# An attention and feed-forward kernel on one core: the order of the first six head pairs, three borrowed buffers, and an earlier load of the last rows

## The chip, the core and the metric

The kernel runs on one core of a Trainium2 chip. A core has TensorE (matrix products), VectorE, ScalarE and GpSimd (elementwise work and reductions), each with its own instruction queue, and SyncE, which here only issues DMAs. Engines run side by side and wait for one another through semaphores; each queue is worked off in order. In the profile's rows they are PE (PEld for its weight loads), DVE, ACT, POOL and SP. The metric is the time of one execution in microseconds (us), as the median of several runs.

## The reference

```python
def rmsnorm(x, g):
    rms = np.sqrt(np.mean(x * x, axis=-1, keepdims=True) + 1e-06)
    return x / rms * g
q_n, k_n = (rmsnorm(q, g_q), rmsnorm(k, g_k))           # (8, 12, 448, 64) each
scores = np.matmul(q_n, k_n.transpose(0, 1, 3, 2)) / np.sqrt(64)
attn = softmax(scores)                                  # max taken off, 1e-09 added to the sum
attn_out = np.matmul(attn, v)
x = attn_out.transpose(0, 2, 1, 3).reshape(8 * 448, 768)
xn = x / np.sqrt(np.mean(x * x, -1, keepdims=True) + 1e-06) * rms_g
g = xn @ w_gate                                         # 768 x 1536
out = (g / (1 + np.exp(-g)) * (xn @ w_val)) @ w_out     # w_out 1536 x 768
```

[...] 

## The kernel before, in words

A sequence has 12 heads, worked on as 6 pairs; there are 48 pairs in all, and the loop of the main program runs over them with the number g. A head's 448 rows are three full tiles of 128, and a rest of 64. The rests of all pairs of a sequence are loaded together (`load_rests`, L430): query rests in one half of the partitions, key rests in the other.

For each pair: `load_pair` (L409, L412) loads the full tiles of q and k. `squares` (L478, L481) squares them on ScalarE and sums on VectorE; `rms_qk` (L497, L498) takes the power -0.5 on GpSimd; `norm_q` (L503) scales the query, on VectorE for pairs 0 and 1 and on GpSimd from pair 2 on. Keys are not scaled: their factor goes into the scale of the exponential. `norm_rests` (L446 to L458) does squares, sums, power and scaling of the rests of two or three pairs at a time. `turn(g, i)` (L519, L523) transposes query (i = 0, with the rest) or key (i = 1) on TensorE; ScalarE copies the turned query qT (L524) and VectorE the turned key kT (L525 its last 64 columns, L527 the others). `score` (L537, L541) multiplies, and ScalarE takes the exponentials; `rests` (L567 to L582) does the 64 last keys and opens the accumulation of the values av (L573) and, for the first seven pairs, of the denominators den (L578). `values` (L589) and `sums` (L602) finish them; VectorE takes the reciprocal (L606) and the product x (L617). av has a single PSUM buffer, so pair g's av starts after pair g - 1's product.

The order on every engine is written out by hand. `pe(fn)` counts a step of TensorE, runs fn, and then all that is due; `after(n, fn)` makes fn due n steps later.

The first seven pairs have no feed-forward work beside them. From pair 7 on, `fill` puts feed-forward products (ff) between the attention steps: L1109 for sequence 0, L991 for its output, L890 and L1081 for the sequences after it, which save products by sums of blocks.

The weights are converted in 72 pieces, one per `convert()`, a pipeline by turns: turn n loads raw piece n (L719), splits piece n - 3 on ScalarE (`split`, L728 and L729), joins piece n - 4 on VectorE (`join`, L734 to L736), adds piece n - 5 on GpSimd into its slot w (L773), and stores piece n - 7 (L761). raw has 7 buffers, top (between split and add) has 4. Before the change the first pairs have four turns at g = 0, and three at each of g = 1 to 6, mostly one by one: one ahead of the next pair's turning, one behind the values, one at the end. From pair 7 on each feed-forward item brings a turn.

Of the kernel before, what the change touches and what calls it, by code (L numbers as in the profile page):

```python
# [8 lines left out]
F32 = mybir.dt.float32  # L9
I32 = mybir.dt.int32  # L10
# [15 lines left out]
BW = 384  # L26
# [309 lines left out]
def safe_scores(  # L336
# [63 lines left out]

    FULL, LAST = slice(0, NK * 128), slice(NK * 128, S)

    def load_pair(g):

        if g >= NG:
            return
        b, hp = divmod(g, NPAIR)
        qk = st["qk", g] = qk_pool.tile([128, 2, 2 * NK * D], F32, name="qk")
        nc.sync.dma_start(out=qk[:, 0].rearrange("p (h n) -> p h n", h=2),  # L409
                          in_=q[b, 2 * hp:2 * hp + 2, FULL].rearrange("h (p t) d -> p h (t d)", t=NK))  # L410
        for h in range(2):
            nc.sync.dma_start(out=qk[:, 1].rearrange("p (t h d) -> p h t d", h=2, d=D)[:, 1 - h],  # L412
                              in_=k[b, 2 * hp + h, FULL].rearrange("(p t) d -> p t d", t=NK))

# [24 lines left out]
    def norm_rests(b, lo, hi):  # L439

        if b >= B:
            return
        n = hi - lo
        rest = st["rest", b][:, lo:hi]
        sq = tmp.tile([128, n, 2, D], F32, name="sq", tag="sq", bufs=2)
        nc.scalar.activation(sq, rest, ACT.Square)  # L446
        ms = small.tile([128, n, 2], F32, name="msr")
        after(1, lambda: nc.vector.tensor_reduce(out=ms, in_=sq, axis=AX_X, op=ALU.add))

        first = b == lo == 0  # L450

        def root():
            nc.gpsimd.tensor_scalar(ms, ms, D * 1e-6, None, ALU.add)
            nc.gpsimd.tensor_tensor(ms, ms, mhalf[:, 0:2 * n].rearrange("p (n h) -> p n h", h=2), ALU.pow)

        def scale():

            (nc.vector if first else nc.gpsimd).tensor_tensor(rest, rest, ms.unsqueeze(3).to_broadcast([128, n, 2, D]), ALU.mult)  # L458

        after(1 if b == 0 else 2, root)  # L460
        if first:
            return scale
        after(1 if b == 0 else 2, scale)

    def direct(g):

# [2 lines left out]
    def squares(g, i):  # L469

        if g >= NG:
            return
        n = 2 * NK
        if i == 0:
            st["ms", g] = small.tile([128, 2 * n], F32, name="ms")
        ms = st["ms", g]
        sq = tmp.tile([128, n * D], F32, name="sq", tag="sq", bufs=2)
        nc.scalar.activation(sq, st["qk", g][:, i], ACT.Square)  # L478

        def reduce():  # L480
            nc.vector.tensor_reduce(out=ms[:, i * n:(i + 1) * n], in_=sq.rearrange("p (n d) -> p n d", d=D), axis=AX_X, op=ALU.add)  # L481

        after(1, reduce)
        if g <= 1:

            after(1, lambda: rms_qk(g, slice(i * n, (i + 1) * n)))
            if i == 0:
                after(1, lambda: norm_q(g))
        elif i == 1:
            after(2, lambda: rms_qk(g))  # L490
            after(2, lambda: norm_q(g))

    def rms_qk(g, cols=slice(0, 4 * NK)):
        if ("rs", g) not in st:
            st["rs", g] = small.tile([128, 4 * NK], F32, name="rs")
        ms = st["ms", g][:, cols]
        nc.gpsimd.tensor_scalar(ms, ms, D * 1e-6, None, ALU.add)  # L497
        nc.gpsimd.tensor_tensor(st["rs", g][:, cols], ms, mhalf[:, cols], ALU.pow)  # L498

    def norm_q(g):  # L500
        qn = st["qn", g] = qn_pool.tile([128, 2 * NK * D], F32, name="qn")
        for h in range(2):
            (nc.vector if g <= 1 else nc.gpsimd).tensor_tensor(  # L503
                qn.rearrange("p (t h d) -> p h t d", h=2, d=D)[:, 1 - h], st["qk", g][:, 0].rearrange("p (h t d) -> p h t d", h=2, d=D)[:, h],
                st["rs", g][:, h * NK:(h + 1) * NK].unsqueeze(2).to_broadcast([128, NK, D]), ALU.mult)

# [212 lines left out]
        nc.sync.dma_start(out=raw.rearrange("p (a n w) -> p a (n w)", a=a, w=2).bitcast(I64), in_=src)  # L719
        return raw  # L720

    def split(raw):


        words = raw.rearrange("p (n w) -> p n w", w=2)
        lo, hi = words[:, :, 0], words[:, :, 1]
        top = cv_pool.tile([128, BW], I32, name="top")
        nc.scalar.activation(top.bitcast(F32), hi.bitcast(F32), ACT.Abs)  # L728
        nc.scalar.activation(lo, lo.bitcast(U32), ACT.Copy, scale=2.0**-29)  # L729
        return lo, hi, top  # L730
# [32 lines left out]
    def convert():  # L763

        n = turn_of["n"]
        if n >= TURNS or not room(1):
            return False
        turn_of["n"] += 1
        if 0 <= n - 5 < len(pieces):
            key = pieces[n - 5][0]  # L770
            st[key] = block()
            lo, top = st.pop(("cv", n - 5))
            nc.gpsimd.tensor_tensor(data(key).bitcast(I32), top, lo, ALU.add)  # L773
        if 0 <= n - 4 < len(pieces):
            st["cv", n - 4] = join(*st.pop(("cv", n - 4)))
        if 0 <= n - 3 < len(pieces):
            st["cv", n - 3] = split(st.pop(("raw", n - 3)))
        if n < len(pieces):
            st["raw", n] = load_raw(pieces[n][1])
        if 0 <= n - 7 < len(pieces):  # L780
            keep(pieces[n - 7][0])
        if turn_of["n"] == TURNS:

            free_w.extend(cv_pool.tile([128, BW], F32, name="top") for _ in range(2))
            whole = [raw_pool.tile([128, 2 * BW], F32, name="raw") for _ in range(7)]
            room_so.extend(whole[:6])
            homes = [whole[6][:, 0:BW], whole[6][:, BW:]] + [cv_pool.tile([128, BW], F32, name="top") for _ in range(2)]
            carried.extend(t[:, i * 128:(i + 1) * 128] for t in homes for i in range(3))
        return True
# [387 lines left out]
        todo.extend(items + (out_items(b) if b == B - 1 else []))  # L1177


    load_pair(0)  # L1180
    load_rests(0, 0, nc.scalar)
    load_rests(0, 1, nc.sync)
    load_pair(1)
    ident = const.tile([128, 128], F32, name="ident")
    make_identity(nc, ident)
# [20 lines left out]
    def gains():  # L1206


        nc.vector.scalar_tensor_tensor(gqk, gq, D**0.5, gk, ALU.mult, ALU.mult)
        nc.vector.tensor_scalar(gqk, gqk, SAFE, -SAFE, ALU.min, ALU.max)  # L1210
# [25 lines left out]
    def turns(n):  # L1236

        for _ in range(n):
            convert()


    squares(0, 0)
    warm(9)
    pe(idle)
    scale = norm_rests(0, 0, 2)
    squares(0, 1)
    after(1, scale)
    pe(lambda: turn(0, 1))
    gains()
    squares(1, 0)  # L1250
    squares(1, 1)
    warm(5)
    pe(lambda: turn(0, 0))
    for g in range(NG + 1):
        b, hp = divmod(g, NPAIR)
        if g:
# [5 lines left out]
        if g == 0:  # L1262
            pe(lambda: score(0, (0,)))
            pe(lambda: rests(0))
            pe(lambda: score(0, (1, 2)))
            pe(lambda: turn(1, 0))
            squares(2, 0)
            squares(2, 1)
            pe(lambda: turn(1, 1))
            norm_rests(0, 2, 4)  # L1270
            for _ in range(3):
                convert()
            load_pair(3)
            load_v(2)
            convert()
            load_rows()
            continue
        if g <= NPAIR:
            pe(lambda: score(g, (0,)))
            squares(g + 2, 0)  # L1280
            squares(g + 2, 1)
            turns(g < NPAIR)
            if g > 1:
                pe(lambda: turn(g + 1, 0))
                some_rests(g)
                pe(lambda: turn(g + 1, 1))
            pe(lambda: rests(g))
            pe(lambda: values(g - 1))
            if g == 1:
                pe(lambda: turn(g + 1, 0))  # L1290
                some_rests(g)
                pe(lambda: turn(g + 1, 1))
            load_v(g + 2)
            turns(g < NPAIR)
            pe(lambda: sums(g - 1))
            pe(lambda: score(g, (1, 2)))
            turns(1 if g < NPAIR else 3)
            if g == 2:
                bound()
            continue  # L1300
# [78 lines left out]
```

## Time and profile before

| What | us |
|---|---|
| median of 4 runs | 1600.4 (1600.18 to 1601.86) |
| the profiled execution, its own time | 1601.51 |
| its span | 1599.7 |
| TensorE busy, share of the span | 1573.5 (98%) |
| VectorE, GpSimd, ScalarE busy | 878.5, 660.3, 470.2 |
| first feed-forward product starts | 101.58 |
| VectorE busy in 0 to 10, 10 to 20, 20 to 30, 30 to 40 | 3.19, 3.65, 5.70, 9.76 |
| ScalarE waits for GpSimd's add before a split, 18 to 280, in all | 34.6 (12 times) |

Busy time of TensorE is taken from records of pipelined products, whose ends are modelled; a stretch that shows as full can have slack in it. So its pace is read from how many products lie in a stretch. A row of a timeline gives the start, the length, the engine, the line of the code, what is written from what, the shape, how many in a row, and in brackets the idle time before it with what ended it. The granted clock of TensorE is 1.00 in nearly all stretches; in 12 to 13, 13 to 14, 14 to 15 and 15 to 16 us it is 0.58, 0.50, 0.50 and 0.72.

### The profile page before, as it was taken

The page shows a single profiled execution, that of the slowest core. Times are in us where ns is not written, and L with a number is a line of the kernel's source. Part 1 is how long each engine was busy: PE and PEld are TensorE (multiplying, and loading weights), DVE is VectorE, ACT ScalarE, POOL GpSimd, SP SyncE. Part 2 cuts the span into 40 slices and gives each one's busy share as a digit, 9 for nine tenths or more (in the row PEclk, how much of TensorE's full clock was granted, in tenths as well). Part 3 has the DMA queues.
Part 4 walks back from the last instruction along what each step waited for, and adds up shares of the span by engine and source line. Part 5 has one row for each costly group of instructions (what it writes and reads, how often), then busy time and mean ns, then how long its engine had stood idle before and what let it go on. Part 6 is the DMA issues. An engine that isn't in the chain of part 4 may idle for free.

```text
span 1599.7 us, 21567 instructions
## 1 busy us (share of the span) xinstructions
PE 1573.5 (98%) x7286; PEld 1114.6 (70%) x7286; DVE 878.5 (55%) x1553; ACT 470.2 (29%) x940; POOL 660.3 (41%) x715
## 2 busy tenths in 40 slices
PE   8999999999999999999999999999999999999998
PEld 4344445787756887568875788667885688859974
DVE  5989889578833556325562354635563355513531
ACT  6746564232222222222222222323322222101010
POOL 6867887555424443344433443344542342000000
PEclk9999999999999999999999999999999999999999
DMA  7748574866756554465544755584554554457652
GB/s 203 213 138 253 177 235 131 280 204 218 255 159 194 154 151 134 134 202 153 155 122 137 209 153 154 149 259 131 163 149 123 172 141 137 124 165 220 174 152 58
DMA packets 261996, 273.28 MB, mean 171 GB/s; under 512 B 78836, under 2 KB 258804, under 8 KB 261876
## 3 DMA queue, kind: packets, MB, share of 16 engines
q1 hardware_dynamic: 260948, 271.61, 57.4%
q8 instruction: 60, 0.98, 0.3%
q14 instruction: 60, 0.49, 0.1%
q10 hardware_dynamic: 800, 0.20, 0.1%
q0 software_dynamic: 128, 0.00, 0.0%
HBM read 232.40 MB, written 39.32 MB: 170 GB/s over the span
## 4 chain that ended last, share of the span: by engine, by line
PE 80%; DVE 5%; issue 1%; POOL 0%; DMA 0%; SPq 0%; ACT 0%; DVEq 0%; POOLq 0%
PE ff L890 40%; PE ff L1081 22%; PE sc L537 6%; PE av L589 5%; PE sc L567 2%; PE den L602 2%; PE tr L519 1%; PE ff L991 1%; DVE top L735 1%; DVE top L736 1%; DVE top L734 0%; PE ff L1109 0%; DVE h L913 0%; DVE rd L610 0%; DVE h L912 0%
## 5 line engine op out<-in xcount | busy, mean ns | idle before, releaser
L890 PE MATMUL ff<-x,w 128*128 128x224 f32 x1878 | 381.5, 354 | 3.7 <-DVE h L913 2.6
L890 PEld LDWEIGHTS ff<-x,w 128*128 128x128 f32 x1878 | 351.3, 190 | 19.2 <-issue 11.7
L547 POOL TENSOR_TENSOR es<-e 128x448 f32<-128x448 f32 x82 | 91.6, 1138 | 491.7 <-ACT e L541 491.7
L890 PE MATMUL ff<-xs,w 128*128 128x224 f32 x1374 | 281.4, 353 | 2.9 <-DVE w L846 2.9
L890 PEld LDWEIGHTS ff<-xs,w 128*128 128x128 f32 x1374 | 258.1, 190 | 6.3 <-issue 6.0
L554 POOL TENSOR_TENSOR es<-es,e 64x448 f32<-64x448 f32 (+1 forms) x164 | 191.8, 1180 | 6.3
L610 DVE RECIPROCAL rd<-rd 128x448 f32<-128x448 f32 x41 | 121.0, 2952 | 109.8 <-ACT rd L609 109.8
L541 ACT ACTIVATE e<-sc,rs 128x448 f32<-128x448 f32 x288 | 161.6, 633 | 49.0 <-PE sc L537 46.7
L1081 PE MATMUL ff<-w,h 128*128 128x384 f32 x498 | 167.8, 487 | 0.6 <-ACT p L1060 0.6
L1081 PE MATMUL ff<-w,raw 128*128 128x384 f32 x468 | 159.5, 487 | 0.3 <-DVE y L1053 0.3
L537 PE MATMUL sc<-qT,kT 64*128 64x448 f32 x576 | 139.2, 575 | 3.4 <-ACT sq L478 1.9
L1081 PEld LDWEIGHTS ff<-w,h 128*128 128x128 f32 x498 | 93.5, 190 | 64.5 <-issue 1.3
L1081 PEld LDWEIGHTS ff<-w,raw 128*128 128x128 f32 x468 | 87.6, 190 | 60.9 <-issue 2.6
L589 PE MATMUL av<-e,vt 128*64 128x448 f32 x576 | 118.8, 548 | 0.0
L498 POOL TENSOR_TENSOR rs<-ms,mhalf 128x12 f32<-128x12 f32 (+1 forms) x50 | 114.4, 2289 | 4.2
L537 PEld LDWEIGHTS sc<-qT,kT 64*128 64x128 f32 x576 | 54.8, 187 | 85.5 <-issue 69.2
L1109 PE MATMUL ff<-x,w 128*128 128x448 f32 x288 | 111.8, 541 | 0.0
L902 DVE TENSOR_TENSOR cc<-ff,u 128x448 f32<-128x448 f32 x84 | 52.3, 623 | 91.7 <-PE ff L890 91.5
L773 POOL TENSOR_TENSOR w<-top,raw 128x384 int32<-128x384 int32 x72 | 77.3, 1088 | 36.5 <-DVE top L736 20.0
L589 PEld LDWEIGHTS av<-e,vt 128*64 128x64 f32 x576 | 37.1, 136 | 75.6 <-issue 75.6
L1109 PEld LDWEIGHTS ff<-x,w 128*128 128x128 f32 x288 | 53.3, 190 | 50.8 <-issue 49.0
L623 POOL TENSOR_TENSOR ss<-ss,rd 128x448 f32<-128x448 f32 x40 | 46.8, 1170 | 79.5 <-ACT rd L622 79.5
(127 smaller groups left out, 1810.9 us busy)
## 6 DMA issues: line engine op xcount, KB each, us to landing
w<-kept SPq DMA_DIRECT2D x511, 192.0 KB, 2.7
w<-kept_o SPq DMA_DIRECT2D x296, 192.0 KB, 2.9
kept<-w SPq DMA_DIRECT2D x89, 192.0 KB, 3.9
qk<-in_q_dram SPq DMA_DIRECT2D x48, 192.0 KB, 3.1
qk<-in_k_dram SPq DMA_DIRECT2D x96, 96.0 KB, 3.5
vt<-in_v_dram SPq DMA_DIRECT2D x48, 192.0 KB, 2.5
raw<-in_moe_w_gate_dram SPq DMA_DIRECT2D x24, 384.0 KB, 4.4
raw<-in_moe_w_val_dram SPq DMA_DIRECT2D x24, 384.0 KB, 5.0
```

The source lines that it names most:

```text
L498: nc.gpsimd.tensor_tensor(st["rs", g][:, cols], ms, mhalf[:, cols], ALU.pow)
L537: nc.tensor.matmul(ps[:, 0:S], lhsT=kT[r, c * 128:(c + 1) * 128], rhs=qT[r, :], start=True, stop=True)
L541: nc.scalar.activation(e, ps[:, 0:S], ACT.Exp, scale=rs[:, n:n + 1])
L547: nc.gpsimd.tensor_tensor(es, st["e", g, 0, j], st["e", g, 1, j], ALU.add)
L554: nc.gpsimd.tensor_tensor(es[r], es[r], e[r], ALU.add)
L589: nc.tensor.matmul(av[own(j), 0:S], lhsT=vt[:, j, c], rhs=st["e", g, c, j], start=False, stop=(c == NK - 1), skip_group_check=True)
L610: nc.vector.reciprocal(rd, rd)
L773: nc.gpsimd.tensor_tensor(data(key).bitcast(I32), top, lo, ALU.add)
L890: nc.tensor.matmul(bank[:, w * HT:(w + 1) * HT], lhsT=wt[:, c * 128:(c + 1) * 128], rhs=x[:, c, :], start=onto is None and w == c == 0, st ...
L902: nc.vector.tensor_tensor(add[name], ps[:, 0:S], add[other], ALU.add)
L1081: nc.tensor.matmul(ps, lhsT=left_o(b, which, LEFT_O[name], c), rhs=data(("wo", b, name, c)), start=first and c == 0, stop=c == NFP - 1, sk ...
L1109: nc.tensor.matmul(bank[w][:, 0:S], lhsT=data(key)[:, c * 128:(c + 1) * 128], rhs=st["x", 0, half][:, c, :], start=half == c == 0, stop=ha ...
```

## The change

- SP loads the key rests of sequence 0 between the first pair's q and its k, where they came behind both.
- The steps of pairs 0 and 1 at the start are put in a fixed order: sums of the rests' squares at once; the query scaled as soon as its own power is there (`squares` hands back its steps for these pairs).
- Pair 1's query is turned between the second and the third tile of pair 0's scores, where it was behind them; the rests of pairs 2 and 3 are squared ahead of pair 2's squares.
- Pair 2's query and the rests of pairs 2 and 3 are scaled on VectorE, where GpSimd did it; pair 2's power goes ahead of the rests' power.
- The conversion's turns of a pair stand together: one behind the values and two at the end for g = 1, and three behind the values and `load_v` for g = 2 to 5. g = 6 has three at the end in both.
- Of each seven pieces up to number 23, three (n % 7 of 4, 5, 6) use a buffer of the pool `c_xs` (three buffers, first needed for the sums of sequence 1, L672) for top.

TensorE's instructions are the same but for two products and four transposes that change places. Three scaling instructions, two for the query of pair 2 and one for the rests, move from GpSimd to VectorE; all else stays on its engine.

```diff
-    def load_pair(g):
+    def load_pair(g, parts=(0, 1)):
...
     def norm_rests(b, lo, hi):
...
-        after(1, lambda: nc.vector.tensor_reduce(out=ms, in_=sq, axis=AX_X, op=ALU.add))
-
+        reduce = lambda: nc.vector.tensor_reduce(out=ms, in_=sq, axis=AX_X, op=ALU.add)
         first = b == lo == 0
+
+        engine = nc.vector if b == 0 and lo < 4 else nc.gpsimd
...
-            (nc.vector if first else nc.gpsimd).tensor_tensor(rest, rest, ms.unsqueeze(3).to_broadcast([128, n, 2, D]), ALU.mult)
-
-        after(1 if b == 0 else 2, root)
+            engine.tensor_tensor(rest, rest, ms.unsqueeze(3).to_broadcast([128, n, 2, D]), ALU.mult)
+
         if first:
+            reduce()
+            root()
             return scale
-        after(1 if b == 0 else 2, scale)
+        after(1, reduce)
+        wait = 2 if lo == 2 else 1
+        after(wait if b == 0 else 2, root)
+        after(wait if b == 0 else 2, scale)
...
     def squares(g, i):
...
+        if g <= 1:
+
+            return reduce, lambda: rms_qk(g, slice(i * n, (i + 1) * n))
         after(1, reduce)
-        if g <= 1:
-
-            after(1, lambda: rms_qk(g, slice(i * n, (i + 1) * n)))
-            if i == 0:
-                after(1, lambda: norm_q(g))
-        elif i == 1:
+        if i == 1:
+            if g == 2:
+
+                due[0:0] = [(now["t"] + 2, lambda: rms_qk(g)), (now["t"] + 2, lambda: norm_q(g))]
+                return
             after(2, lambda: rms_qk(g))
             after(2, lambda: norm_q(g))
...
     def norm_q(g):
-            (nc.vector if g <= 1 else nc.gpsimd).tensor_tensor(
+            (nc.vector if g <= 2 else nc.gpsimd).tensor_tensor(
...
-    def split(raw):
+    def split(raw, n):
...
-        top = cv_pool.tile([128, BW], I32, name="top")
+        if n < 24 and n % 7 > 3:
+
+            top = s_pool.tile([128, 3, HT], I32, name="xs")[:, 0:2].rearrange("p c n -> p (c n)")[:, 0:BW]
+        else:
+            top = cv_pool.tile([128, BW], I32, name="top")
...
-    load_pair(0)
+    load_pair(0, (0,))
     load_rests(0, 0, nc.scalar)
     load_rests(0, 1, nc.sync)
+    load_pair(0, (1,))
     load_pair(1)
...
-    squares(0, 0)
+    def at_once(steps):
+        for step in steps:
+            step()
+
+    at_once(squares(0, 0))
     warm(9)
-    pe(idle)
+    norm_q(0)
     scale = norm_rests(0, 0, 2)
-    squares(0, 1)
-    after(1, scale)
+    steps = squares(0, 1)
     pe(lambda: turn(0, 1))
+    at_once(steps)
+    scale()
     gains()
-    squares(1, 0)
-    squares(1, 1)
+    at_once(squares(1, 0))
+    reduce, root = squares(1, 1)
     warm(5)
     pe(lambda: turn(0, 0))
+    reduce()
+    norm_q(1)
+    root()
...
             pe(lambda: rests(0))
-            pe(lambda: score(0, (1, 2)))
+            pe(lambda: score(0, (1,)))
             pe(lambda: turn(1, 0))
+            pe(lambda: score(0, (2,)))
+            norm_rests(0, 2, 4)
             squares(2, 0)
             squares(2, 1)
             pe(lambda: turn(1, 1))
-            norm_rests(0, 2, 4)
...
             squares(g + 2, 1)
-            turns(g < NPAIR)
             if g > 1:
...
             load_v(g + 2)
-            turns(g < NPAIR)
+
+            turns(1 if g == 1 else 3 if g < NPAIR else 0)
             pe(lambda: sums(g - 1))
             pe(lambda: score(g, (1, 2)))
-            turns(1 if g < NPAIR else 3)
+            turns(2 if g == 1 else 3 if g == NPAIR else 0)
```

More of the change, by code (lines that the diff above doesn't have):

```diff
@@ L407, in load_pair @@
         b, hp = divmod(g, NPAIR)
[L408 to L411, printed above, removed]
+        if 0 in parts:
+            qk = st["qk", g] = qk_pool.tile([128, 2, 2 * NK * D], F32, name="qk")
+            nc.sync.dma_start(out=qk[:, 0].rearrange("p (h n) -> p h n", h=2),
+                              in_=q[b, 2 * hp:2 * hp + 2, FULL].rearrange("h (p t) d -> p h (t d)", t=NK))
+        qk = st["qk", g]
+        for h in range(2) if 1 in parts else ():
             nc.sync.dma_start(out=qk[:, 1].rearrange("p (t h d) -> p h t d", h=2, d=D)[:, 1 - h],
@@ L776, in convert @@
         if 0 <= n - 3 < len(pieces):
-            st["cv", n - 3] = split(st.pop(("raw", n - 3)))
+            st["cv", n - 3] = split(st.pop(("raw", n - 3)), n - 3)
         if n < len(pieces):
```

## The prediction

> **What bounds the kernel now.** I read the windows of each stretch first, then the timelines of TensorE, VectorE and GpSimd up to 110 us. Pairs are counted from 0; x(g) is the scaled output of pair g (L617), kT(g), qT(g) its turned keys and queries.
>
> From TensorE's timeline, start and length in us:
> ```profile
> 54.37 0.97 PE L573 MATMUL av<-e,vr 64*64 64x448 f32 x4
> ...
> 56.02 2.48 PE L589 MATMUL av<-e,vt 128*64 128x448 f32 x12
> 58.32 2.42 PE L602 MATMUL den<-e,ones 128*64 128x448 f32 x12
> 60.68 2.31 PE L537 MATMUL sc<-qT,kT 64*128 64x448 f32 x8
> ...
> 97.69 0.60 PE L649 MATMUL rb<-ident,rs 112*128 112x112 f32 x4 [1.03 <-POOL rs L641]
> ...
> 99.17 2.48 PE L602 MATMUL den<-e,ones 128*64 128x448 f32 x12
> 101.58 7.03 PE L1109 MATMUL ff<-x,w 128*128 128x448 f32 x18
> ```
> From 101.58 on TensorE is the bound: 18 records in 7.03 us, 0.39 each, and the same pace in every such group up to 252, with 0.43 and 0.82 us of idle at 205 and 245. What VectorE does after 101.58 costs next to nothing, however full it is (24.41 of 26 us in 101 to 127). So the change is worth what it moves the start of the first ff. The edits that matter lie ahead of it.
>
> Ahead of it VectorE and a loop through TensorE share the bound:
> ```profile
> 18.28 0.22 DVE L525 COPY kT<-tr 128x64 f32<-128x64 f32 x1 [3.66 <-ACT qT L524]
> ...
> 26.88 0.22 DVE L525 COPY kT<-tr 128x64 f32<-128x64 f32 x1 [3.61 <-ACT qT L524]
> ...
> 49.36 0.35 DVE L734 TENSOR_SCALAR top<-top 128x384 f32<-128x384 f32 x1
> 49.74 0.36 DVE L735 TENSOR_SCALAR top<-top 128x384 int32<-128x384 int32 x1
> 50.14 0.56 DVE L736 SCALAR_TENSOR_TENSOR top<-raw,top 128x384 int32<-128x384 int32 x1
> ...
> 54.14 0.35 DVE L734 TENSOR_SCALAR top<-top 128x384 f32<-128x384 f32 x1
> 54.52 0.87 DVE L735 TENSOR_SCALAR top<-top 128x384 int32<-128x384 int32 x1
> 55.42 1.25 DVE L736 SCALAR_TENSOR_TENSOR top<-raw,top 128x384 int32<-128x384 int32 x1
> ...
> 86.04 2.96 DVE L606 RECIPROCAL rd<-den 128x448 f32<-128x448 f32 x1 [2.42 <-PE den L602]
> 89.03 0.62 DVE L617 TENSOR_TENSOR x<-av,rd 128x448 f32<-128x448 f32 x1
> ```
> ```profile
> 20.32 2.30 POOL L498 TENSOR_TENSOR rs<-ms,mhalf 128x12 f32<-128x12 f32 x1
> 22.69 0.97 POOL L503 TENSOR_TENSOR qn<-qk,rs 128x192 f32<-128x192 f32 x2
> ...
> 25.18 0.61 POOL L458 TENSOR_TENSOR rest<-rest,msr 128x256 f32<-128x256 f32 x1
> ...
> 48.93 2.30 POOL L498 TENSOR_TENSOR rs<-ms,mhalf 128x12 f32<-128x12 f32 x1
> ...
> 54.13 1.04 POOL L458 TENSOR_TENSOR rest<-rest,msr 128x384 f32<-128x384 f32 x1
> 55.14 3.51 POOL L773 TENSOR_TENSOR w<-top,raw 128x384 int32<-128x384 int32 x3
> ```
> See three things. VectorE idles 3.66 and 3.61 us before kT(1) and kT(2). One turn's join (L734 to L736) takes 1.3 us at 49.36, beside GpSimd's power, and 2.5 at 54.14, beside GpSimd's scaling and adds; the next one takes 3.7. And there is a loop: x(2) ends at 54.22, the next av starts at 54.37 (one PSUM buffer), its sums end at 60.74, 6.5 later; reciprocal and product take 3.7 more, so no pair is shorter than 10.2 us. The x rows end at 32.67, 43.24, 54.22, 67.02, 79.40, 89.65: the pairs that end at 67.02 and 79.40 are the long ones, 12.8 and 12.4.
>
> **The change part by part.** I place the rows' durations in the new order; each time is "before -> estimate".
>
> *Rests before the first k.* Each takes two issues, 1.3 us. The rests, used at 7.18, land at about 6.0. The query's scaling on VectorE (6.52 to 7.15) now stands ahead of their sums, so: sums 7.1 to 7.5, GpSimd 0.24 and 1.04 to 8.96, scaling 0.43, transpose 10.02 -> 9.5, qT, first score 11.07 -> 10.55. The k lands 1.3 later (transposes 6.05 -> 7.2); its root ends at 10.75 and the first exponential wants it at 11.66, so that is covered by 0.9. Gain 0.5. Past the k moved behind them nothing else on SP's queue changes place.
>
> *Turn(1,0) before the third scores.* qn(1) is scaled as soon as its own root is there (12.55), no longer behind a reduction. ScalarE copies qT(1) between the exponentials, 17.60 -> 15.45, and kT(1) no longer waits for all of them; score(1) 19.12 -> 17.55.
>
> *Third pair.* Its squares stay behind the last exponentials (17.2) and the rests' square, so sums end 19.90 -> 19.15 and the 2.30 root 22.62 -> 21.9. Then the chain is shorter: VectorE takes qn(2) (0.63) beside GpSimd's 0.24 and 1.04, then the rests (0.43), where GpSimd needed 0.97, 0.24, 1.04 and 0.61 in a row. kT(2) 26.88 -> 24.9. The 1.06 us put on VectorE lies in its idle time there.
>
> *Conversion.* The first join (20.36, in that idle time) goes behind kT(2), where VectorE is full: 1.3 paid. x(0) 32.67 -> 30.8; kT(3) 36.87 -> 35.05 with one join fewer done. From here three joins follow kT and stand before the reciprocal. By x(1) six are done instead of five: x(1) 43.24 -> 44.8, later. In pairs 3 and 4 they now run beside GpSimd's powers (2.30 and 1.35), not its scaling and adds, which go beside the reciprocal (2.95 in every row, also at 86.04 beside qn at 85.95). I charge one clash of 0.7 to 0.8 with qn per group: three joins 4.6 instead of 7.3. x(2) 54.22 -> 55.6, limited by joins.
>
> New wait: kT(5) now stands first behind x(2), but qT(5) comes behind six exponentials (3.2), two squares (0.95) and the copy, from sums ending at 51.3: kT(5) at 57.2, VectorE idle 1.6. Then reductions 1.0, copy 0.5, rests' sums 0.55, joins 4.6, reciprocal and product 3.6: x(3) 67.02 -> 67.6. The last two pairs go by the loop, 10.25 each (the joins fit, with 0.2 and 2.7 to spare): x(4) 79.40 -> 77.9, x(5) 89.65 -> 88.05. All 15 joins are done at x(5) in both orders. From x(5) to the first ff the order is the same, 11.9 us: ff 101.58 -> 100.0.
>
> *Buffers and queues.* ScalarE waits 34.6 us in all for GpSimd to free top; with seven buffers that goes up to piece 23, but it frees no path: VectorE had work. The three borrowed buffers are next written at 262.43, so nothing waits for them. SP takes vt ahead of the three raw loads, which wait for values; they land in 4.4 to 5.0 and are split a pair (10 us) later. Both at nothing; without this cover a split would come up to 2 us late once per pair.
>
> Sum: 1.6 us off. The profiled execution took 1601.51 (span 1599.7), 1.1 above the median; I take the shift off the median: 1598.8.
>
> **Unknown prices.** (a) Clock: it is 0.58, 0.50, 0.50 and 0.72 in the four microseconds from 12, after idle at 9 to 11. TensorE now idles 1.7 instead of 0.5 before the first transposes and less later. Between no slow stretch (1.5 less) and a second one as long (1.5 more); I take no difference, the row being there in both orders. (b) Joins: 1.3 clean to 3.7 each; I take 4.6 per three, near the clean rows since only qn overlaps.
>
> Against the change speaks the Trainium skill, "SBUF — State Buffer", "Who interferes with whom": a GpSimd instruction holds the port pair it shares with VectorE for its whole length and blocks two-input and two-port work. Taken by that alone, joins beside the powers would stall, by an estimate from that page, for four powers of 2.3 and two of 1.35 us, and the sum would be some 12 us worse. The rows from 49.36 to 50.70, a join at full speed inside the power of 48.93 to 51.23, differ, and I follow them.
>
> **The rivals.**
> - *More is gained:* the slow clock stretch vanishes (1.5), or exponentials run ahead so that kT(5) does not wait (1.6). One or both: 1595.7 to 1597.3. For it: both waits are artefacts of single rows; against: ScalarE's order puts qT behind.
> - *The start gives it back:* a second slow stretch takes 1.5 from the 1.6: 1600.3.
> - *Slower:* the grouped joins meet GpSimd's adds. The place is pairs 3 and 4, where GpSimd needs 10.7 us per pair (2.3, 0.97, 1.6, 1.04, 3.5, 1.2) and falls behind. A group at the old 7.3 costs 2.7 more. In pair 3 the wait before kT(5) takes up 1.6 of it, so pairs 3 and 4 together cost 1.1 and 2.7: 1602.6; with pair 5 too, whose slack is 0.2, 2.5 more: 1605.1. It decides from 3.2 us of clash above what I charge over joins 6 to 11, half of it for the wait and half for the gain. Against: GpSimd starts each pair at the reductions, which now come first.
> - *The buffers change nothing:* ScalarE's waits were never on the path; that is already in my sum.
>
> **How the numbers follow.** About 0.2% (3.2 us, 1597.2 to 1603.6) is what can be told from no change. Forecast 0.50 (own range 1597.5 to 1600), more gained 0.25, start gives back 0.12, slower rival 0.13. Faster: 0.22 of the second and 0.06 of the first's edge, 0.28. Slower: the rival's upper half, 0.07. The range leaves out the ends of the second and the last: 1595.6 to 1601.8.
>
> **What would show it.** First score near 10.5; kT(2) near 25; VectorE idle before kT(5), waiting for ScalarE's qT; joins of 1.3 us beside the powers; x(5) near 88; first ff near 100. Wrong if joins in pairs 3 and 4 average above 2 us, if the clock row at 12 to 16 moves or doubles, or if TensorE idles after 101 for weights.

## The result and the profile after

| | kernel before | changed kernel |
|---|---|---|
| median, us | 1601.49 (1600.0 to 1602.1) | 1599.63 (1598.2 to 1600.5) |
| ratio to before | 1 | 0.9989, 95% interval 0.9984 to 0.9993 |
| profiled execution, its own time | 1601.51 | 1598.41 |
| its span | 1599.7 | 1596.6 |
| first ff starts | 101.58 | 98.01 |

The change makes the kernel about 1.8 us faster (1.1 to 2.6 by the interval). The interval keeps clear of no change, but the gain is smaller than the 0.2% that the prediction took for the least that can be told from it. In about half of the executions of either kernel TensorE's clock is halved for some 3 us during the first 16, so that the times of each kernel lie in two groups about 1.6 us apart. Before: 1600.0 to 1600.6 and 1601.5 to 1602.1. Changed: 1598.2 to 1598.6 and 1599.6 to 1600.5. Group by group the change is worth 1.8 and 1.7 us by the middles. The profile of before has that stretch and the profile of after has not; so of the 3.57 us between the two first ffs about 1.45 is clock. A later experiment (the buffers alone) left a profile of the old order without the stretch, and it is the fair partner of the profile after. (Its first three transposes take 0.88 us, where 0.52 is usual; the wait for the scaled rest takes that up, and its first score comes at 11.14.) Below, "old order, even clock" means that one.

| start of kT, end of x, start of ff (us) | kT(2) | x(0) | x(1) | x(2) | x(3) | x(4) | x(5) | first ff |
|---|---|---|---|---|---|---|---|---|
| before | 26.88 | 32.67 | 43.24 | 54.22 | 67.02 | 79.40 | 89.65 | 101.58 |
| old order, even clock | 25.41 | 31.20 | 41.77 | 52.76 | 65.57 | 77.94 | 88.20 | 100.13 |
| changed | 24.44 | 30.23 | 43.50 | 53.81 | 65.38 | 75.76 | 86.09 | 98.01 |

TensorE's timeline of the changed kernel (start, length, engine, line, what is written from what, shape, count, and the idle time before with what ended it):

```profile
7.11 0.52 PE L527 MATMUL tr<-ident,qk 128*128 128x128 f32 x3 [1.68 <-DMA qk<-in_k_dram]
7.47 1.28 PE L1240 MATMUL warm<-ident 128*128 128x128 f32 x10
8.58 0.49 PE L527 MATMUL tr<-ident,qn 128*128 128x128 f32 x3
8.91 1.28 PE L1240 MATMUL warm<-ident 128*128 128x128 f32 x10
10.03 0.27 PE L531 MATMUL tr<-ident,rest 128*128 128x128 f32 x1
11.03 1.02 PE L545 MATMUL sc<-qT,kT 64*128 64x448 f32 x4 [0.72 <-ACT qT L532]
...
98.01 7.03 PE L1121 MATMUL ff<-x,w 128*128 128x448 f32 x18
```

The same stretch before the change:

```profile
6.05 0.52 PE L519 MATMUL tr<-ident,qk 128*128 128x128 f32 x3 [0.54 <-DMA qk<-in_k_dram]
10.02 0.33 PE L523 MATMUL tr<-ident,rest 128*128 128x128 f32 x1 [0.89 <-DVE rest L458]
11.07 1.02 PE L537 MATMUL sc<-qT,kT 64*128 64x448 f32 x4 [0.72 <-ACT qT L524]
```

The first score starts at 11.03, where it started at 11.07 before. The rest's transpose used to wait 0.89 us for the scaled rest; now it waits for nothing, but stands behind the late k's transposes, the query's and two groups of warm-up products of 1.28 us, and so starts at the same time, 10.03. The ff group has the old length, 7.03 for 18.

VectorE's timeline of the changed kernel, from kT(2) on:

```profile
24.44 0.22 DVE L533 COPY kT<-tr 128x64 f32<-128x64 f32 x1 [0.17 <-ACT qT L532]
...
39.90 2.95 DVE L614 RECIPROCAL rd<-den 128x448 f32<-128x448 f32 x1
42.88 0.62 DVE L625 TENSOR_TENSOR x<-av,rd 128x448 f32<-128x448 f32 x1
...
45.95 0.34 DVE L746 TENSOR_SCALAR xs<-xs 128x384 f32<-128x384 f32 x1
46.32 0.36 DVE L747 TENSOR_SCALAR xs<-xs 128x384 int32<-128x384 int32 x1
46.71 0.56 DVE L748 SCALAR_TENSOR_TENSOR xs<-raw,xs 128x384 int32<-128x384 int32 x1
...
48.45 0.66 DVE L746 TENSOR_SCALAR top<-top 128x384 f32<-128x384 f32 x1
49.15 0.55 DVE L747 TENSOR_SCALAR top<-top 128x384 int32<-128x384 int32 x1
49.73 0.56 DVE L748 SCALAR_TENSOR_TENSOR top<-raw,top 128x384 int32<-128x384 int32 x1
50.20 2.95 DVE L614 RECIPROCAL rd<-den 128x448 f32<-128x448 f32 x1
...
55.65 0.23 DVE L533 COPY kT<-tr 128x64 f32<-128x64 f32 x1 [1.84 <-ACT qT L532]
...
82.48 2.96 DVE L614 RECIPROCAL rd<-den 128x448 f32<-128x448 f32 x1 [3.34 <-PE den L610]
```

GpSimd's timeline of the changed kernel, beside those joins and behind them:

```profile
45.75 2.30 POOL L506 TENSOR_TENSOR rs<-ms,mhalf 128x12 f32<-128x12 f32 x1
48.13 1.35 POOL L511 TENSOR_TENSOR qn<-qk,rs 128x192 f32<-128x192 f32 x2
...
52.36 1.99 POOL L785 TENSOR_TENSOR w<-xs,raw 128x384 int32<-128x384 int32 x2
54.30 1.02 POOL L785 TENSOR_TENSOR w<-top,raw 128x384 int32<-128x384 int32 x1
```

Four things are to be seen. The idle time right before kT(2), 3.61 us before the change, is 0.17; a little ahead of it VectorE still idles 2.76 and 0.97 us, before the scaling of the query and of the rests. A join (the VectorE part of turning the weights, which arrive as 64-bit floats, into 32-bit ones) beside the power (45.95 to 47.27) takes 1.3 us; the one beside the scaling of qn (48.45 to 50.20) takes 1.75; the adds come at 52.36, beside the product and the wait before kT(5). That wait, 1.84 us for ScalarE's qT, is new; kT(6) and kT(7) wait 0.72 and 1.76 as well. And before the reciprocal of pair 5 VectorE idles 3.34 us: there is room there.

Of the 2.12 us between the two first ffs at even clock, 0.4 is lost at the very end: from VectorE's last step on the output to the end of the span it is 6.01 us in the old order and 6.39 in the changed one. This end is about 6.0 or about 6.4 in every profile here, and it does not follow any one edit: all with the old start have 6.0, but those with the new start have both (5.96 with the rests loaded late, 6.48 with the turns one by one). I leave its cause open.

### The profile page after: what moved, and what is told of

Read it like the earlier page. It is cut to its first block, busy times and chain, and to the rows that moved or that the text cites. A ratio compares the mean times of both kernels' runs of the same rounds, so it can differ in the third digit from the quotient of the medians.

```text
span 1596.6 us, 21562 instructions
## 1 busy us (share of the span) xinstructions
PE 1571.3 (98%) x7286; PEld 1113.4 (70%) x7286; DVE 872.6 (55%) x1556; ACT 469.9 (29%) x940; POOL 658.6 (41%) x712
## 4 chain that ended last, share of the span: by engine, by line
PE 79%; DVE 6%; DMA 1%; POOL 0%; issue 0%; SPq 0%; ACT 0%; DVEq 0%; POOLq 0%
PE ff L902 40%; PE ff L1093 22%; PE sc L545 6%; PE av L597 5%; PE sc L575 2%; PE den L610 2%; PE tr L527 1%; DVE top L747 1%; DVE top L748 1%; DVE top L746 1%; PE ff L1003 1%; DVE rd L618 1%; DVE h L925 0%; DVE h L924 0%; POOL w L785 0%
## 5 line engine op out<-in xcount | busy, mean ns | idle before, releaser
L914 DVE TENSOR_TENSOR u<-ff,p 128x448 f32<-128x448 f32 x42 | 26.1, 622 | 96.8 <-PE ff L902 96.8
```

The source lines that it names most:

```text
L914: nc.vector.tensor_tensor(add[name], ps[:, 0:S], add[other], ALU.add)
```

## The experiments

They are grouped by the part of the change that they test. Times are given as the range without the half-clock stretch and the range with it.

### The conversion's turns together, with the old start

The kernel before, with the grouped turns and the three borrowed buffers, and nothing of the new start.

```diff
-        top = cv_pool.tile([128, BW], I32, name="top")
+        if n < 24 and n % 7 > 3:
+            top = s_pool.tile([128, 3, HT], I32, name="xs")[:, 0:2].rearrange("p c n -> p (c n)")[:, 0:BW]
+        else:
+            top = cv_pool.tile([128, BW], I32, name="top")
...
             squares(g + 2, 1)
-            turns(g < NPAIR)
...
-            turns(g < NPAIR)
+            turns(1 if g == 1 else 3 if g < NPAIR else 0)
             pe(lambda: sums(g - 1))
             pe(lambda: score(g, (1, 2)))
-            turns(1 if g < NPAIR else 3)
+            turns(2 if g == 1 else 3 if g == NPAIR else 0)
```

> The kernel before with only the turns put together and the three buffers. My forecast: 0.4 us slower than before, since a join moves from VectorE's idle time behind kT(2), and the wait for qT and the loop take what the shorter joins save. Rival (the conversion carries the gain): 1.5 us or more faster than before, with joins of three at some 4.4 us in pairs 3 and 4.

Measured: 1598.5 to 1598.9 and 1600.1 to 1600.5, ratio 0.9992 (0.9983 to 1.0001). The interval mixes the groups and touches 1; by the middles of the groups it is 1.5 us under the kernel before and about 0.2 over the changed one. My forecast (0.4 slower) was wrong here and the rival right. Its profile has the stretch: kT(2) 26.99 and first ff 100.25, against 26.88 and 101.58 before. So the grouped turns with their buffers carry nearly all of the gain in time; the whole new start adds 0.2 to 0.3 us. At the first ff the new start is worth more: 100.25 less the 1.58 by which the stretch delays kT(2) here (26.99 for 25.41) is, as an estimate, 98.67, against 98.01. Some 0.4 of this is lost again at the end of the span.

### The new start, with the turns one by one

The changed kernel with four buffers for top and the old places of the turns.

```diff
             squares(g + 2, 1)
+            turns(g < NPAIR)
...
-            turns(1 if g == 1 else 3 if g < NPAIR else 0)
+            turns(g < NPAIR)
...
-            turns(2 if g == 1 else 3 if g == NPAIR else 0)
+            turns(1 if g < NPAIR else 3)
```

> The changed kernel with the conversion's turns one by one again and four buffers for top; the new start stays. My forecast had the start bring 2.0 us at kT(2) and the conversion give 0.4 of it back: then this one is 0.4 us faster than the changed kernel, some 2 us faster than before, with x(5) at least 2 us ahead of the kernel before. Rival: the start's gain is swallowed by the full VectorE, and the shorter joins of pairs 3 and 4 (7.3 to some 4.4 us for three) carry the gain: then this one is within 0.3 us of before.

Measured: 1601.4 to 1601.9 and 1603.2 to 1603.7, ratio 1.0010 (1.0001 to 1.0019): about 1.5 us slower than before by the middles of the groups. Neither the forecast (2 us faster than before) nor the rival (within 0.3) came. VectorE's timeline of this kernel:

```profile
21.17 0.63 DVE L511 TENSOR_TENSOR qn<-qk,rs 128x192 f32<-128x192 f32 x2 [2.76 <-POOL rs L506]
22.77 0.43 DVE L460 TENSOR_TENSOR rest<-rest,msr 128x256 f32<-128x256 f32 x1 [0.98 <-POOL msr L457]
23.12 0.35 DVE L742 TENSOR_SCALAR top<-top 128x384 f32<-128x384 f32 x1
...
25.30 0.21 DVE L533 COPY kT<-tr 128x64 f32<-128x64 f32 x1
...
45.80 1.37 DVE L744 SCALAR_TENSOR_TENSOR top<-raw,top 128x384 int32<-128x384 int32 x1
47.09 0.21 DVE L533 COPY kT<-tr 128x64 f32<-128x64 f32 x1
```

And the same engine in the old order at even clock:

```profile
18.88 0.38 DVE L738 TENSOR_SCALAR top<-top 128x384 f32<-128x384 f32 x1
...
25.41 0.22 DVE L525 COPY kT<-tr 128x64 f32<-128x64 f32 x1 [3.60 <-ACT qT L524]
...
45.92 0.21 DVE L525 COPY kT<-tr 128x64 f32<-128x64 f32 x1
```

In the old order the first join (18.88) lies in VectorE's idle time before kT(2), for nothing. In the new one VectorE idles 2.76 and 0.98 us there, but the join stands behind the scalings that wait for GpSimd, so it runs at 23.12, ahead of the sums and kT(2), and delays them: kT(2) 25.30 instead of 24.44. Later joins meet GpSimd's work in other places (45.80: 1.37 us instead of 0.56, beside an instruction of GpSimd from 45.44 to 46.75), and x(2) ends at 53.92 against 52.76. From there on both orders take the same time per pair (12.81, 12.38 and 10.26 here; 12.81, 12.37 and 10.26 there): first ff 101.30 against 100.13.

### The same, with the first join moved behind kT(2)

```diff
             squares(g + 2, 1)
-            turns(g < NPAIR)
+            turns(1 < g < NPAIR)
...
-            turns(1 if g < NPAIR else 3)
+            turns(2 if g == 1 else 1 if g < NPAIR else 3)
```

The lines taken away are those of the experiment before this one.

> The changed kernel's start with the old four top buffers and the turns one by one, as in the first run of this study, but the first turn of pair 1 stands at the end of that pair instead of ahead of kT(2). If the first run lost the start's gain because this join stood ahead of kT(2) (24.44 there became 25.30), kT(2) is back near 24.4, x(0) ends near 30.2, and the rest follows with the old spacing: first ff near 99.2 on a clean clock, lower group of times near 1599.3. If it lost it in pairs 2 and 3, where joins met GpSimd's adds in a new place (kT(3) 35.75 against 35.40, kT(4) 47.09 against 45.92), the gain at x(0) is used up again by x(2), first ff 100.3 to 101.3, lower group 1600.3 to 1601.4.

Measured: 1601.9 to 1602.2 in ten executions and 1606.25 in one, for which no run gives a reason; ratio 1.0007 (0.9998 to 1.0016), first ff 101.67. The profile, at 1602.18, is without the half-clock stretch, so the ten stand against the lower group of the kernel before on the same chip (1600.1 to 1600.4): 1.8 us slower, and slower than both expectations. kT(2) is indeed back at 24.41 and x(0) at 30.21, as the first theory said. But now three joins instead of two stand between x(0) and kT(3), which comes at 36.17 instead of 35.40, and x(2) ends at 54.33. The second theory gave the outcome's sign, but most of the loss needs no new clash: from x(0) to x(1) it is 12.33 us instead of 10.57, and a third join of 1.96 stands there, one step of it beside an add. VectorE is full from kT(2) to x(2), and the join that once lay in idle time cost time in both places in which it was put: 0.86 us at kT(2) in the run before this one, 1.76 from x(0) to x(1) here.

### The grouped turns without the buffers

The changed kernel with four buffers for top.

```diff
-        if n < 24 and n % 7 > 3:
-            top = s_pool.tile([128, 3, HT], I32, name="xs")[:, 0:2].rearrange("p c n -> p (c n)")[:, 0:BW]
-        else:
-            top = cv_pool.tile([128, BW], I32, name="top")
+        top = cv_pool.tile([128, BW], I32, name="top")
```

> The changed kernel with top in four buffers for all pieces. My forecast put the buffers at nothing: the changed kernel's time within 0.3 us. Rival: with three turns together the third split waits for the add of the first turn of its group, which ends at 53.35, 65.3 and 73.5 us in pairs 3 to 5 of the changed kernel, and ScalarE's six exponentials, which began at 51.02, 61.47 and 72.90, stand behind it: 2.4 and 3.8 us later in pairs 3 and 4, 2 to 7 us slower in all.

Measured: 1612.1 to 1613.6, ratio 1.0079 (1.0065 to 1.0093): about 13.5 us slower than the changed kernel. My forecast (nothing) was wrong; the rival has the mechanism, and half the size. ScalarE's timeline of this kernel:

```profile
51.45 0.57 ACT L737 ACTIVATE raw<-raw 128x384 int32<-128x384 uint32 x1
58.14 0.55 ACT L736 ACTIVATE top<-raw 128x384 f32<-128x384 f32 x1 [6.12 <-POOL w L781]
58.60 0.53 ACT L737 ACTIVATE raw<-raw 128x384 int32<-128x384 uint32 x1
59.03 2.19 ACT L549 ACTIVATE e<-sc,rs 128x448 f32<-128x448 f32 x4
```

and VectorE's:

```profile
48.48 0.23 DVE L533 COPY kT<-tr 128x64 f32<-128x64 f32 x1 [2.83 <-ACT qT L532]
...
64.13 0.23 DVE L533 COPY kT<-tr 128x64 f32<-128x64 f32 x1 [5.91 <-ACT qT L532]
...
79.79 0.22 DVE L533 COPY kT<-tr 128x64 f32<-128x64 f32 x1 [5.31 <-ACT qT L532]
```

The third split of a group waits 6.12 us for GpSimd to free a buffer, and behind it in ScalarE's queue stand the exponentials (59.03 here; 51.02 in the changed kernel), and behind these qT, for which kT(4), kT(5) and kT(6) wait 2.8 to 5.9 us. The first ff starts at 113.21 instead of 98.01; 1.6 us of this is the half-clock stretch, which this profile has (kT(2) 26.04 for 24.44).

### The buffers alone

The kernel before with the three borrowed buffers; the turns stay one by one and the start stays old. The edit is the first part of the diff of the first experiment.

> The kernel before with the three borrowed buffers for top alone; the turns stay spread and the start stays old. If the buffers matter only as room for grouped turns, this is the kernel before: 1600.2 to 1601.7, x(5) near 89.6, first ff near 101.5. If a part of the gain is the buffers by themselves (splits that no longer wait for GpSimd's adds), 0.5 to 1.5 us faster, first ff near 100.5.

Measured: 1600.0 to 1600.3 and 1601.2 to 1601.9, ratio 1.0001 (0.9992 to 1.0010): the kernel before. By themselves the buffers are worth nothing; with the grouped turns they are worth about 13.5 us. Its profile is the even-clock reference in the table above.

### The first k loaded first again

```diff
-    load_pair(0, (0,))
+    load_pair(0)
     load_rests(0, 0, nc.scalar)
     load_rests(0, 1, nc.sync)
-    load_pair(0, (1,))
```

> The changed kernel with the key rests loaded behind the first k again. My forecast gave this edit 0.5 us: 0.5 us slower than the changed kernel, first score 0.5 later. Rival: the first score waits for something else (the warm-up products ahead of the rest's transpose, then qT) and the time stays within 0.2 us. On the clock: TensorE idles 0.5 instead of 1.7 us before the first transposes; if that idle time made the stretch at half clock, it comes less often here.

Measured: 1598.2 to 1598.5 and 1599.7 to 1600.0, ratio 0.9987 (0.9978 to 0.9996), first score at 11.13: the changed kernel, as the rival had it. The place of this load is worth nothing: here the rest's transpose waits 1.18 us for the scaled rest and starts at 10.08, and in the changed kernel it stands behind TensorE's queue until 10.03. On the clock this run decides nothing: 4 of 11 executions are in the upper group, and the idle time has only moved, from before the first transposes (0.41 us here, 1.68 in the changed kernel) to before the rest's.

### The third pair's scaling back on GpSimd

```diff
-        engine = nc.vector if b == 0 and lo < 4 else nc.gpsimd
+        engine = nc.vector if b == 0 and lo < 2 else nc.gpsimd
...
-            (nc.vector if g <= 2 else nc.gpsimd).tensor_tensor(
+            (nc.vector if g <= 1 else nc.gpsimd).tensor_tensor(
```

> The changed kernel with the query of pair 2 and the rests of pairs 2 and 3 scaled on GpSimd again, in the new order. My forecast: the chain to kT(2) is GpSimd 0.97 longer for the query and 0.2 for the rests, so kT(2) and all behind it 1.2 us later, up to the first ff: 1.2 us slower than the changed kernel. Rival: a later kT(2) is taken up by VectorE's idle time before kT(5) and kT(7) (1.84 and 1.76 us in the changed kernel): within 0.3 us.

Measured: 1598.9 in two executions, 1600.2 to 1600.6 in eight and 1601.9 in one; ratio 0.9998 (0.9989 to 1.0007). By the middles of the groups that is 0.2 to 0.5 us slower than the changed kernel. At even clock kT(2) starts at 25.53, after an idle wait of 4.18, and the first ff at 98.79: 1.09 and 0.78 later. So VectorE's scaling accounts for the whole move of kT(2), as forecast; in the times the rival is nearer. Its place was another, though: the waits before kT(5) and kT(7) stay (1.85 and 1.75), 0.3 us is taken up between x(0) and x(1), and as much at the end of the span (6.04 for 6.39).

### Pair 1's query turned behind the scores

```diff
-            pe(lambda: score(0, (1,)))
+            pe(lambda: score(0, (1, 2)))
             pe(lambda: turn(1, 0))
-            pe(lambda: score(0, (2,)))
```

> The changed kernel with pair 1's query turned behind all of pair 0's scores again. My forecast: qT(1) comes behind two more exponentials (1.17 us), but the root of pair 2 still follows its squares, which are behind the exponentials in both, so kT(2) moves by 0.5 at most: 0 to 0.5 us slower than the changed kernel. Rival: score(1) comes 1.2 us later and everything with it: 1.2 us slower.

Measured: 1598.5 to 1599.3 and 1600.2 to 1600.9, ratio 0.9989 (0.9980 to 0.9998). The groups begin 0.3 and 0.6 us above the changed kernel's and overlap with them; the ratio is the same. This piece is worth a few tenths at most, and these runs do not settle how many.

### More warm-up products at the start

In the changed kernel, seven more products at the start, and three between the rest's transpose and the first score.

```diff
-    warm(9)
+    warm(16)
...
+            if g == 0:
+                warm(3)
             nc.scalar.activation(st["qT", g], ps[:, 0:S], ACT.Copy, scale=gqk[:, 0:1])
```

> The changed kernel with more warm-up products in TensorE's idle time at the start: seven ahead of the first transposes, three between the rest's transpose and the first score. The times of the kernels before and after fall into two groups each, 1.5 to 1.7 us apart. If the upper group is the one with the granted clock near a half for some 3 us at 12 to 16 us, as in the profile of before, and idle time of TensorE ahead of it is the cause, all times here fall into the lower group, near 1598.4. If the groups come from elsewhere, both stay, as often as in the changed kernel.

Measured: 1598.5 to 1599.3, all executions; ratio 0.9987 (0.9978 to 0.9996). The group near 1600 is gone. The first score is 0.36 us later (11.39), and the best times are 0.3 us above those of the changed kernel. The same in the kernel before:

```diff
-    warm(9)
+    warm(11)
...
-                warm(5)
+                warm(9)
...
+            if g == 0:
+                warm(3)
```

> The kernel before, with more warm-up products ahead of its first transposes and first score, nothing else. If the half-clock stretch after TensorE's idle time at the start is what parts the kernel before into times near 1600.2 and times near 1601.7, then the upper ones vanish: all runs within 1600.0 to 1600.7, and the profile shows a clock of 1.00 from 10 us on. If something else makes the two groups, both stay and the median lies between 1600.2 and 1601.9.

Measured: ten of eleven executions at 1600.1 to 1600.7 and one at 1601.4, while 13 of 27 of the kernel before, on the same chip, lay above 1601.4; ratio 0.9997 (0.9988 to 1.0006). So the two groups are the clock, and they come from TensorE's idle time at the start, as was expected; not without any exception in the old order. What shows it is the three kernels with more warm-up products together (these two and the last one below): one of 33 executions is in an upper group. Eleven executions of one kernel would not do: with the first join moved behind kT(2), TensorE idles 1.88 us before 7.09, and yet ten of eleven executions lie within 0.3 us.

### Two joins moved into idle time

In the changed kernel, one turn instead of three behind the values of pair 2, and two behind those of pair 6, where VectorE idled 3.34 us before the reciprocal of pair 5.

```diff
-            turns(1 if g == 1 else 3 if g < NPAIR else 0)
+            turns({1: 1, 2: 1, NPAIR: 2}.get(g, 3))
```

> The changed kernel with two turns of pair 2's group moved to pair 6, ahead of its sums, where VectorE idles 1.76 and 3.34 us. If VectorE's five joins are what makes x(0) to x(1) 13.27 us long, against 10.3 in the loop through TensorE, x(1) comes 2.5 us earlier and the whole is 2 to 2.5 us faster than the changed kernel. Rival: the wait for qT, which follows six exponentials, holds the next pairs all the same (x(1) to x(3) stays at 21.9 us or grows), or the two joins make pair 6 longer: less than 0.5 us.

Measured: 1596.2 to 1596.6 and 1597.7 to 1598.2, ratio 0.9976 (0.9967 to 0.9985): 2 us under the changed kernel. Its profile has the half-clock stretch. TensorE's timeline at its start:

```profile
7.17 0.87 PE L527 MATMUL tr<-ident,qk 128*128 128x128 f32 x3 [1.60 <-DMA qk<-in_k_dram]
7.83 2.34 PE L1240 MATMUL warm<-ident 128*128 128x128 f32 x10
9.96 0.85 PE L527 MATMUL tr<-ident,qn 128*128 128x128 f32 x3
...
12.77 0.65 PE L545 MATMUL sc<-qT,kT 64*128 64x448 f32 x2 [0.72 <-ACT qT L532]
```

After 1.60 us of idle, a group of ten warm-up records takes 2.34 us, where ten take 1.28 in the profile after; the first score is 1.74 us late. The granted clock in the windows of this stretch reads 1.00 all the same: here the slow clock is seen only in the length of the products. That it is the clock is read from another profile: with pair 1's query turned behind the scores, products are stretched in the same place (ten in 2.00 and 1.93 us), and there the granted clock reads 0.50 from 8 to 11.

### Both: the joins moved and the warm-up

> The changed kernel with both edits that helped by themselves: joins moved (one turn behind the values of pair 2 instead of three, two behind those of pair 6) and more warm-up products at the start. If the two are independent, the times are those of the moved joins without their upper group: 1596.2 to 1596.9, 0.25% below the kernel before, first ff near 96. If the warm-up products delay the first score by more than the loop through av and the sums takes up, 1597 to 1598.

The two edits above together. Measured: 1596.4 to 1597.3, median 1596.68, ratio 0.9976 (0.9967 to 0.9985), no group some 1.6 us higher. VectorE's timeline:

```profile
37.42 2.95 DVE L616 RECIPROCAL rd<-den 128x448 f32<-128x448 f32 x1
40.41 0.63 DVE L627 TENSOR_TENSOR x<-av,rd 128x448 f32<-128x448 f32 x1
42.94 0.23 DVE L535 COPY kT<-tr 128x64 f32<-128x64 f32 x1 [1.36 <-ACT qT L534]
...
53.39 0.22 DVE L535 COPY kT<-tr 128x64 f32<-128x64 f32 x1 [0.71 <-ACT qT L534]
...
80.70 2.96 DVE L616 RECIPROCAL rd<-den 128x448 f32<-128x448 f32 x1 [1.30 <-PE den L612]
```

The reciprocal of pair 1 starts 2.48 us earlier than in the changed kernel (37.42 for 39.90), since two joins fewer stand ahead of it. The idle time before the reciprocal of pair 5 shrinks from 3.34 to 1.30: that is where the two joins went. First ff 96.24 instead of 98.01. It is the best kernel of this study: 3.8 us under the kernel before by the medians on the same chip (1600.46), and 1.8 under the changed kernel without the stretch.

## Why the prediction was right in its sum and wrong in its parts

The sum was 1.6 us off the time before; measured were 1.8. (The forecast of 1598.8 went out from the median 1600.4 of four runs; over many it is 1601.49, and the changed kernel comes at 1599.63.) That the sums agree so well is luck: the forecast had the start bring about 2 us and the conversion give 0.3 to 0.4 back, and measured at even clock the start brings 0.97 at x(0) and the conversion adds 1.14 on the way to x(5). One part was put 0.9 us too high, the other 1.4 too low. At even clock, old order against changed:

| step | forecast | measured |
|---|---|---|
| first score | -0.5 | 0 (11.07 to 11.03, profiles before and after) |
| kT(2) | -2.0 | -0.97 |
| x(0) | -1.9 | -0.97 |
| x(1) | +1.6 | +1.73 |
| x(2) | +1.4 | +1.05 |
| x(3) | +0.6 | -0.19 |
| x(4) | -1.5 | -2.18 |
| x(5), first ff | -1.6 | -2.11, -2.12 |

- **The bound held.** From x(5) to the first ff it is 11.92 us in the changed kernel, 11.93 before, and the pace behind it is the same.
- **"Rests before the first k": wrong.** The step "transpose 10.02 -> 9.5" followed the rests alone. The k that lands 1.06 us later holds up its own transposes, those of the query and the warm-up products between, and these stand ahead of the rest's transpose in TensorE's queue. The working looked for who wants the late k's root and not for what is queued behind its transposes.
- **"Turn(1,0) before third scores": the direction was right.** Score(1) starts at 16.66 where it starts at 17.64 in the old order at even clock: 1.0 for the forecast 1.6. Undoing it costs a few tenths of the time at most.
- **"Third pair": right in mechanism, twice too large.** The step "sums end 19.90 -> 19.15" failed. At even clock they end at 18.41 in the old order (first row) and at 18.56 in the changed one (second):

```profile
17.41 1.00 DVE L481 TENSOR_REDUCE ms<-sq 128x6 f32<-128x384 f32 x2
```

```profile
17.41 1.15 DVE L487 TENSOR_REDUCE ms<-sq 128x6 f32<-128x384 f32 x2
```

The working let pair 0's last exponentials end 0.5 us earlier; they end 0.4 later (16.66 for 16.25), since the copy of qT(1), 0.64 us, now stands between them on ScalarE. The half-clock stretch is not the reason: with it in both orders the sums end at 19.89 before and at 20.26 with the first k loaded first. What remained, 0.97, is the shorter chain on VectorE, and the experiment with GpSimd gives 1.09.
- **What the new start is worth: over-rated.** The forecast charged 1.3 for the first join's lost place, and that is what the runs show: with the turns one by one the start loses more than it gains. With grouped turns it gains 0.2 to 0.3 in time, and some 0.7 at the first ff.
- **"Conversion": right in mechanism, its gain put too low by 1.4 us.** Three joins were put at 4.6; from the first one to the reciprocal they take 4.15 in pair 1 and 4.25, 4.14 and 4.55 in the next three, with the one clash with qn as forecast (and a second one in the 4.55). So the pairs that end at x(1), x(2) and x(3) take 13.27, 10.31 and 11.57 us, where the working had 14.0, 10.8 and 12.0; the last two take 0.3 more than it had. The forecast for this part alone was 0.4 slower; with the old start it gains 1.5. Counted from the first step of each join to the end of its third, the 13 joins between x(0) and x(5) took 28.8 us in the old order, and the 14 in the changed one take 22.3; most of these 6.5 us goes into the new waits for qT and the loop. x(1) comes later and x(4) and x(5) earlier, as worked out. The new wait was put at 1.6 us before kT(5) and is 1.84; that kT(6) and kT(7) wait too was not seen, though the pairs in which these waits lie take 10.38 and 10.33 us, near the shortest there is.
- **"Buffers and queues": "frees no path" was wrong.** It holds for the old spacing, as the buffers alone show. With three splits in a row it is the buffers that keep ScalarE's exponentials moving, about 13.5 us. I had costed the buffers in the order in which they are not needed.
- **Unknown (a), the clock:** no difference was taken, and that held over many executions (31 of 60 before and 21 of 40 changed are in the upper group, which lies 1.5 and 1.7 us higher), though the two profiles suggest otherwise. A sign of being wrong came nevertheless, that the clock row at 12 to 16 moves: in the three profiles of the late k that have the stretch it follows the longer idle time before the first transposes and lies between 7 and 12 us. With the k loaded first again it is back at 12 to 16.
- **The rule against the change:** the Trainium skill, "SBUF — State Buffer", "Who interferes with whom", would have a GpSimd instruction block VectorE's two-input work for its whole length. In the changed kernel a whole join, whose third step has two inputs, ran from 45.95 to 47.27 at 0.34, 0.36 and 0.56 us, inside GpSimd's power of 45.75 to 48.05. The page differs from the measurement here, and the measurement decides.

Of the rivals, "more is gained" did not come, but its idea, that the joins and the wait at kT(5) leave something on the table, was right: moving two joins gave 2 us, and the wait before kT(5) fell to 0.71. "Slower" fell, since the adds came at 52.36, behind the joins. "The start gives it back": no second slow stretch came, but the start is worth little all the same, for another reason, a full VectorE.

## What to carry to other kernels

When an engine is made busier in its idle time, look at what used to lie in that idle time: here the first join lost its free place, and the chain that got shorter by 1 us was worth 0.2 to 0.3 in time. Grouping short steps of a side task beside another engine's slow but harmless instruction saved 1.5 us and needed enough buffers, without which the same order cost 13.5 us: cost buffers and order together. And two profiles may differ by the clock of a few microseconds at the start; compare groups of times before giving a difference of the traces to the change.

## What the runs showed of the hardware that I had not expected

- TensorE's half-clock stretch comes in about half of the executions of one and the same program (31 of 60, 21 of 40). It follows idle time in the first 11 us (1.60 us before 7.17 with the joins moved; 0.89 and 0.72 us before 10.02 and 11.07 in the kernel before), lasts about 3 us and costs 1.4 to 1.7 us at the end. With the idle time filled by 128x128 products it was absent from all 22 executions of the changed order (two kernels), and from ten of eleven of the old one. Idle time alone does not bring it each time: after 1.88 us of it (first join moved behind kT(2)) ten of eleven executions are without it.
- A join of 1.3 us keeps its length beside GpSimd's power (128x12, 2.30 us) and takes 1.75 beside a scaling, 2.5 to 3.7 beside scaling and adds (rows before and after).
- The reciprocal (2.94 to 2.96 us) has the same length in every row, whatever GpSimd does beside it.
